# Eight transposes of the identity ahead of the first transposes of the normalised input, in a four-layer attention and convolution kernel

## The chip, the cores and the metric

The kernel runs on one core of a Trainium2 chip. The metric is device time in microseconds (us) of one execution; lower is better. The core's engines each work through their own list of instructions: TensorE (PE, with its weight loads shown as PEld), VectorE (DVE), ScalarE (ACT), GpSimd (POOL) and SyncE (SP), which issues most of the transfers (DMA). They wait for each other through semaphores.

## The reference

The input `x` is 2048 rows of 512 in bf16. Four residual layers follow each other, two of a kind:

```python
x = x + _A_ref(_layernorm(x, axis=-1), A_wqkv, A_wo)
x = x + _B_ref(_layernorm(x, axis=-1), B_A_re, B_A_im, B_B_re, B_B_im, B_C_re, B_C_im, B_log_dt, B_Dskip)
x = x + _A_ref(_layernorm(x, axis=-1), A_wqkv, A_wo)
x = x + _B_ref(_layernorm(x, axis=-1), B_A_re, B_A_im, B_B_re, B_B_im, B_C_re, B_C_im, B_log_dt, B_Dskip)
```

`_A_ref` is attention with 32 heads of 16 over a window of 8 keys that lie 2 rows apart: projections to q, k and v, logits, a softmax over the 8 keys, the weighted sum of v, and a projection by `A_wo`. `_B_ref` builds, from complex parameters, a kernel K of 2048 taps for each of the 512 channels, convolves each channel of its input with it (through a transform of length 4096 in the reference), and adds the input times `Dskip`.

## The kernel before

All of the order is written by hand: a string of letters for each stage (`ORDERK`, `CORE0`, `ORDER0`, `ORDERF`, `CORE1`, `ORDER1`) names the operations one after the other, and each engine gets its instructions in that order. Everything is unrolled; there is no loop on the chip.

In order of time the stages are:

- `k_gen` (to about 105 us). VectorE and ScalarE build the tables of the convolution kernel. TensorE first transposes the parameters (`turned_by`, line 1048), then has nothing until the input is normalised. Between the table work stands the front of the first attention layer: ScalarE takes the sums of the input block `x_blk`, normalises it (line 195), TensorE transposes it (`turn`, line 1213) into a PSUM tile `pt`, ScalarE copies that to `xnT` (line 1216), and TensorE projects k and q (`proj`, line 1223).
- `core` of the first attention layer. Each of the 16 blocks of 128 rows has a product of the attention weights with v on VectorE (`pv_mult`, line 472, tile `pav`), a sum of it on TensorE by 64 small multiplies with the identity (`pv_sum`, line 497, tile `po`), a copy on ScalarE (line 499), the output projection (`out_proj`, lines 506 and 508) and its copy with the sums of the next layer norm (lines 514 and 145).
- The convolution of the first layer as a transform in two steps (`FftB`: lines 810, 821, 828, 865, 877, 891, 895, 939 to 945).
- The same two for the second layers (`ORDERF` and `CORE1` up to about 343 us, then `ORDER1`).

The change touches `turn` inside `k_gen`. It is called eight times, for four blocks b and two halves d of their columns, each time with a new tile from the PSUM pool `ps_tr` of two buffers. The calls are listed under the key `t` of the operations. The identity `ident` is made by GpSimd at the start and already serves the transposes of the parameters.

Every multiply or transpose on TensorE is two instructions, a weight load and the multiply. Line 1213 waits for ScalarE's line 195 row by row.

Of the kernel before, what the change touches and what calls it, by code (L numbers as in the profile page):

```python
# [74 lines left out]
"""  # L75
ROWS0 = (0, 2, 1, 3, 4, 5, 6, 7, 8, 9, 10, 11, 12, 13, 14, 15)
ROWS1 = (0, 2, 1, 3, 4, 5, 6, 7, 8, 9, 10, 11, 12, 13, 14, 15)
NCOL = (4, 3)
ENGK = dict(b="AAAAAAAAAAAAAAAAA", y="AAAAAAAAAAAA", z="AAAA", e="AAAAAAAA", K="AAAAAAAAAAAAAAAA", Q="AAAAAAAA", x="AAAAAAAAAAAAAAAA")
STATD = (3,)  # L80
# [6 lines left out]
def build_a_consts(nc, cpool, tpool, c):  # L87
# [14 lines left out]
    sv = tpool.tile([4, 4, H], I32, name="iota_slot")  # L102
    mc = tpool.tile([4, max(NCOL), W], I32, name="iota_slot_mask")
    ind = cpool.tile([P, NDT * H], BF16, name="ind32")

    def iotas():
        nc.gpsimd.iota(u[:], pattern=[[-16, 8]], base=0, channel_multiplier=1)
        nc.gpsimd.iota(mv[:], pattern=[[1, NA], [-2, W]], base=0, channel_multiplier=0)
        nc.gpsimd.iota(sv[:], pattern=[[-1, 4], [0, H]], base=0, channel_multiplier=1)
        nc.gpsimd.iota(mc[:], pattern=[[4, max(NCOL)], [-2, W]], base=0, channel_multiplier=1)  # L110
        nc.gpsimd.memset(ind[:], 0.0)

    def rest():
# [12 lines left out]
        nc.gpsimd.tensor_scalar(slot[:], sv[:], 0, None, ALU.is_equal)  # L126
        keep = cpool.tile([4, max(NCOL), W], BF16, name="slot_mask")
        nc.gpsimd.tensor_scalar(keep[:], mc[:], 0, -1e9, ALU.is_lt, ALU.mult)
# [71 lines left out]
class LayerA:  # L200


    def __init__(self, tc, nc, consts, lnst, A_wqkv, A_wo, layer, xnT, nq):
        self.tc, self.nc, self.c, self.lnst, self.layer = tc, nc, consts, lnst, layer
        self.ncol = NCOL[layer]
        self.ctx = ExitStack()
# [152 lines left out]
    def core(self, x_sb, u, lnp, order, ev, nprod=0):  # L359
# [9 lines left out]
        with ExitStack() as c2:  # L369
# [184 lines left out]
            blocks = [(q,) for q in range(4)]  # L554
            rows = [(a,) for a in (ROWS1 if l else ROWS0)]
            ops = dict(
# [450 lines left out]
def k_gen(tc, nc, a_consts, ins, kd, la, x_v, lnst, zero, b_consts):  # L1007
# [3 lines left out]
    with ExitStack() as ctx:  # L1011
# [10 lines left out]
        ident = la.c["ident"]  # L1022
# [51 lines left out]
        p_im = turned_by("A_im", by_dt)  # L1074
        p_re = turned_by("A_re", by_dt)
        nc.scalar.mul(nat(turn), p_im, 1.0 / TWO_PI)
        nc.vector.tensor_scalar(t1[:], turn, MAGIC, None, ALU.add)
        nc.vector.scalar_tensor_tensor(turn, t1[:], MAGIC, turn, ALU.subtract, ALU.subtract)
        nc.vector.scalar_tensor_tensor(t2[:], turn, -1.0, turn, ALU.mult, ALU.max)
        nc.scalar.activation(nat(a_re), p_re, ACT.Exp)  # L1080
# [6 lines left out]
        for name, copy in (("B_re", nc.scalar.copy), ("B_im", nc.scalar.copy)):  # L1087
            b = sp.tile([P, 4 * P], BF16, name="in_" + name)
# [119 lines left out]

        def turn(b, d):
            pt = xps[b, d] = la.ps_tr.tile([P, 2, 4, P], BF16, name="pt")  # L1210
            for di in range(2):
                for a in range(4):
                    nc.tensor.transpose(pt[:, di, a, :], xb[b][:, a, (2 * d + di) * P:(2 * d + di + 1) * P], ident[:])  # L1213
# [119 lines left out]
        def calls(f, *args):  # L1333
            return [lambda a=a: f(*a) for a in args]

        def chain(*fs):
# [6 lines left out]
            b=[f for k in range(12) for f in calls(power, (k,)) + (calls(power_neg, (k,)) if 3 <= k <= 7 else [])],  # L1343
# [9 lines left out]
            d=calls(x_load, (2,), (3,)), E=calls(la.front_ext, *((b, "dma") for b in range(3))),  # L1353
# [257 lines left out]
```

## Time and profile before

| | us |
|---|---|
| median of 3 runs | 389.48 |
| lowest and highest | 389.33, 390.03 |
| the profiled execution | 390.78 |
| its span, from its first to its last instruction | 389.0 |

The runs of the table's first two rows are without a profile; the third is the one that the profile's rows come from. The activity of the engines in 40 equal slices of the span, 9.7 us each, in tenths:

```profile
PE   3000267999999999999998999999999999997894
DVE  6999999999999999999999989979999999989984
ACT  7999999898578799999999998764675889989993
```

TensorE has little to do in the first 50 us and much from 65 us on; VectorE is nearly full all along. In rows of the timeline the columns are the start, the time to the end of the group, the engine, the line, the operation with its tiles and sizes, the count, and in brackets the idle time before with what ended it. Rows of the chain that ended last have a start, a length, the engine, tile and line. "issue" is time in which an engine waited for nothing that the profile shows.

### The profile page before, as it was taken

How to read it: one execution, taken by the hardware profiler on the slowest of the kernel's cores; microseconds unless marked ns; L12 is line 12 of the kernel's file. 1: busy time of each engine (PE TensorE's matmuls, PEld its weight loads, DVE VectorE, ACT ScalarE, POOL GpSimd, SP SyncE). 2: the span in 40 equal slices, each digit the busy share in tenths (PEclk: the TensorE clock that was granted, in tenths of full speed). 3: DMA queues.
4: the chain of work that ended last, by engine and by line, in shares of the span. 5: the costliest groups of instructions: out<-in, count | busy, mean ns of one | idle time of the engine just before them, and what ended most of it. 6: DMA issues, size and time to landing. Idle time of an engine off the chain costs nothing.

```text
span 389.0 us, 14544 instructions
## 1 busy us (share of the span) xinstructions
PE 324.6 (83%) x6361; PEld 220.7 (57%) x6361; DVE 369.1 (95%) x439; ACT 338.0 (87%) x581; POOL 63.3 (16%) x97
## 2 busy tenths in 40 slices
PE   3000267999999999999998999999999999997894
PEld 2000125757634455666887898544446666677894
DVE  6999999999999999999999989979999999989984
ACT  7999999898578799999999998764675889989993
POOL 9400980000290000001531200200000010000000
PEclk9999999999999999999999999999999999999999
DMA  7951822114025556287575733077303274404515
GB/s 206 405 172 18 86 73 75 36 35 96 16 66 167 169 168 189 77 231 234 213 273 224 273 112 111 3 264 224 95 0 97 70 237 144 157 3 148 182 55 168
DMA packets 68302, 54.16 MB, mean 139 GB/s; under 512 B 33545, under 2 KB 58670, under 8 KB 67982
## 3 DMA queue, kind: packets, MB, share of 16 engines
q1 hardware_dynamic: 66566, 48.70, 42.4%
q0 software_dynamic: 1664, 4.52, 3.1%
q8 instruction: 50, 0.82, 0.9%
q14 instruction: 14, 0.11, 0.1%
q10 hardware_dynamic: 8, 0.00, 0.0%
HBM read 30.15 MB, written 13.24 MB: 112 GB/s over the span
## 4 chain that ended last, share of the span: by engine, by line
PE 46%; ACT 20%; issue 3%; SPq 2%; DMA 1%; DVE 0%; ACTq 0%
PE pq L398 7%; ACT ub L877 5%; PE pq L223 5%; ACT a1s L810 5%; PE po L497 4%; PE pp L282 4%; PE pq L508 3%; PE L L350 3%; PE pb L821 2%; SPq L597 2%; PE pb L891 2%; PE L L424 2%; PE pb L895 2%; PE pb L940 2%; PE pb L941 1%
## 5 line engine op out<-in xcount | busy, mean ns | idle before, releaser
L472 DVE TENSOR_TENSOR pav<-attn,v_ext 128x4096 bf16<-128x4096 bf16 (+1 forms) x34 | 72.2, 2158 | 0.2 <-PE po L497 0.2
L342 DVE TENSOR_TENSOR prod<-qT,kT_ext 128x4096 bf16<-128x4096 bf16 x29 | 65.4, 2287 | 1.9 <-ACT qT L225 0.6
L1213 PE MATMUL pt<-ident,x_blk 128*128 128x128 bf16 x64 | 6.3, 241 | 39.4 <-ACT x_blk L195 39.4
L1127 DVE TENSOR_TENSOR A_t<-A_t,pow_t 128x1024 bf16<-128x1024 bf16 (+4 forms) x46 | 38.1, 869 | 0.1
L497 PEld LDWEIGHTS <-pav 64*128 64x128 bf16 x1984 | 31.1, 95 | 12.1 <-issue 7.0
L497 PE MATMUL po<-ident,pav 64*128 64x64 bf16 x1984 | 34.7, 190 | 0.7 <-issue 0.5
L508 PE MATMUL pq<-wop,oT 128*128 128x512 bf16 x128 | 32.8, 379 | 0.0
L877 ACT CAST ub<-pb 128x1024 bf16<-128x1024 f32 x32 | 31.7, 1116 | 0.0
L828 PE MATMUL pb<-a1s,w_sb 128*128 128x64 bf16 x768 | 27.7, 193 | 3.6 <-ACT a1s L810 1.9
L810 ACT CAST a1s<-pb 128x1024 bf16<-128x1024 f32 x30 | 29.4, 1054 | 1.4 <-PE pb L821 1.2
L1223 PE MATMUL pp<-xnT,kT_ext 128*128 128x512 bf16 x96 | 26.2, 402 | 4.9 <-ACT kT_ext L1228 2.1
L398 PE MATMUL pq<-wv,xnT 128*128 128x512 bf16 x128 | 30.2, 379 | 0.0
L1213 PEld LDWEIGHTS <-x_blk 128*128 128x128 bf16 x64 | 4.8, 107 | 41.7 <-ACT x_blk L195 40.5
L828 PEld LDWEIGHTS <-w_sb 128*128 128x128 bf16 x768 | 24.9, 98 | 6.0 <-issue 4.3
L400 ACT CAST v_ext<-pq 128x512 bf16<-128x512 f32 x32 | 18.6, 586 | 11.1 <-PE pq L398 10.9
L223 PE MATMUL pq<-xnT,kT_ext 128*128 128x512 bf16 x96 | 24.2, 380 | 0.0
L1285 PEld LDWEIGHTS <-A_t 128*64 128x64 bf16 (+1 forms) x512 | 21.6, 103 | 3.8 <-DVE A_t L1127 0.2
L1285 PE MATMUL pk<-B_t,A_t 128*64 128x84 bf16 (+1 forms) x512 | 23.5, 201 | 0.1
L810 DVE CAST a1s<-pb 128x1024 bf16<-128x1024 f32 x18 | 21.4, 1218 | 1.5 <-PE pb L821 1.1
L499 ACT CAST oT<-po 128x512 bf16<-128x512 f32 x31 | 17.8, 573 | 3.6 <-PE po L497 3.6
L398 PEld LDWEIGHTS <-xnT 128*128 128x128 bf16 x128 | 11.9, 98 | 15.5 <-issue 2.3
L508 PEld LDWEIGHTS <-oT 128*128 128x128 bf16 x128 | 12.5, 98 | 12.6
(262 smaller groups left out, 888.5 us busy)
## 6 DMA issues: line engine op xcount, KB each, us to landing
w_sb<-w_dram SPq DMA_DIRECT2D x64, 128.0 KB, 3.3
w_dram<-xnT SPq DMA_DIRECT2D x1, 4096.0 KB
kf_ring<-kf_dram SPq DMA_DIRECT2D x13, 256.0 KB, 3.9
kf_ring<-kf_dram SPq DMA_DIRECT2D x26, 128.0 KB, 4.3
v_ext<-v_ext SPq DMA_DIRECT2D x4, 784.0 KB, 6.0
x_blk<-in_A_x_dram SPq DMA_DIRECT2D x4, 512.0 KB, 5.3
kT_ext<-in_A_wqkv_dram SPq DMA_DIRECT2D x4, 512.0 KB, 13.1
x_sb<-in_A_x_dram SPq DMA_DIRECT2D x4, 512.0 KB, 6.8
```

Of the source, the lines that this page charges most:

```text
L223: nc.tensor.matmul(pq[:], lhsT=self.wqk[:, dt, ft * P:(ft + 1) * P], rhs=self.xnT[:, dt, q * 512:(q + 1) * 512], start=(dt == 0), stop=(dt ...
L342: nc.vector.tensor_tensor(pr, self.qT[q][:, ft].unsqueeze(1).to_broadcast([P, W, 4, P]), kap, ALU.mult)
L398: nc.tensor.matmul(pp[:], lhsT=xnT[:, dt, a * P:(a + 1) * P], rhs=wv[:, dt, :], start=(dt == 0), stop=(dt == NDT - 1))
L472: nc.vector.tensor_tensor(pv[:, i], attn[:, n % 4].unsqueeze(2).to_broadcast([P, W, DH // parts, H]), vap, ALU.mult)
L497: nc.tensor.matmul(po[:, h, 0, i * nt + ft, :], lhsT=pvf[rows, i, w, ft * P:(ft + 1) * P], rhs=ident[rows, rows], start=(w == 0 and ft + i ...
L508: nc.tensor.matmul(pw[:], lhsT=oT[:, ftp, :], rhs=self.wo[:, ftp, :], start=False, stop=(ftp == NDT - 1))
L810: (self.nc.scalar.copy if eng == "act" else self.nc.vector.tensor_copy)(dst, src)
L828: nc.tensor.matmul(p2[:, j, :], lhsT=self.w2[:, ec * EC + j, :], rhs=a1s[:, ec * EC + j, :], start=True, stop=True)
L877: nc.scalar.copy(ub[:], p2)
L1127: return lambda: nc.vector.tensor_tensor(*args)
L1223: nc.tensor.matmul(pps[kind, b, ft][:], lhsT=la.wqk[:, dt, c:c + P], rhs=la.xnT[:, dt, b * 512:(b + 1) * 512], start=(dt == 0), stop=(dt = ...
L1285: nc.tensor.matmul(o, lhsT=lhs, rhs=Bt[:, ri, c * CH + ql].rearrange("p b g -> p (b g)"), start=(not half and j % 4 == 0 and ri == 0), sto ...
```

## The change

Ahead of the eight transposes of the first call of `turn`, eight transposes of the identity are put into the first place of the same tile, which the first real transpose then overwrites. Nothing reads them.

```diff
+IDLE = 8
...
         def turn(b, d):
             pt = xps[b, d] = la.ps_tr.tile([P, 2, 4, P], BF16, name="pt")
+            for _ in range(IDLE if (b, d) == (0, 0) else 0):
+                nc.tensor.transpose(pt[:, 0, 0, :], ident[:], ident[:])
             for di in range(2):
                 for a in range(4):
```

TensorE's list grows by 16 instructions; the other engines' lists keep theirs in the same order.

## The prediction

> **What bounds the kernel now.** I read the busy shares first, then the chain that ended last, then the costliest groups for the line that changes.
>
> ```profile
> PE 324.6 (83%) x6361; PEld 220.7 (57%) x6361; DVE 369.1 (95%) x439; ACT 338.0 (87%) x581; POOL 63.3 (16%) x97
> PE 46%; ACT 20%; issue 3%; SPq 2%; DMA 1%; DVE 0%; ACTq 0%
> L1213 PE MATMUL pt<-ident,x_blk 128*128 128x128 bf16 x64 | 6.3, 241 | 39.4 <-ACT x_blk L195 39.4
> q8 instruction: 50, 0.82, 0.9%
> ```
>
> Three engines are nearly full and hand the bound to each other: VectorE is busy 95% of the span, TensorE carries 46% of the chain, ScalarE 20%. The third row is the group the change touches: TensorE idles 39.4 us ahead of the transposes of the normalised input, waiting for ScalarE. The fourth is what the change can reach later: 50 instruction packets, 0.82 MB, so 16.4 KB each. TensorE has 6361 multiplies and 6361 weight loads, 12722 instructions; 12722 / 50 = 254 for a packet. So one packet a block of about 256 TensorE instructions. Every engine's other instructions stand in the same order after the change, but all 16 added ones (a weight load with each transpose) push the later code 16 places on, so each block now ends 8 multiplies earlier in the program.
>
> **The direct cost.** The next view is TensorE's order of time around the inserted place, and the engine totals of the stretch.
>
> ```profile
> 7.02 0.60 PE L1048 MATMUL pt<-dt_diag,raw_C_im 128*128 128x128 bf16 x4 [0.76 <-DMA raw_C_im<-in_B_C_im_dram]
> 45.02 0.29 PE L1213 MATMUL pt<-ident,x_blk 128*128 128x128 bf16 x1 [37.40 <-ACT x_blk L195]
> 47.14 1.57 PE L1213 MATMUL pt<-ident,x_blk 128*128 128x128 bf16 x13 [0.42 <-ACT x_blk L195]
> 45.00:54.20 9.20, 6.44 (x26) 3.02 (x27) 9.20 (x16) 9.20 (x18) 9.20 (x1) 1.00 0.62 111
> ```
>
> The eight transposes read only the identity, so they carry no wait: they start when the last transposes of `raw_C_im` are through, at about 7.6 us, and not at 45 us. Thirteen transposes back to back take 1.57 us, 0.12 us each, so eight take about 1 us and end near 8.7 us. The next work on TensorE starts at 45.02 us. Cover: 36 us of idle. Direct cost 0; without that cover it would be 1 us. They write a tile whose first reader waits for the later real transposes, so nobody waits for them; no DMA is added, and no queue is passed.
>
> **The indirect cost: where the blocks end.** I searched the bursts of equal small multiplies for a gap that no wait explains. There are two. The view is the chain in order of time, then the timeline: TensorE's weight loads and multiplies, and two rows of ScalarE behind them.
>
> ```profile
> 310.10 1.04 PE po L497 x64
> 311.14 0.89 PE L L354 x32
> 312.03 0.13 PE L L332
> 312.16 0.55 PE L L459 x8
> 312.71 0.63 PE po L497 x36
> 313.35 0.47 issue
> 313.82 0.58 PE po L497 x28
> ...
> 322.89 0.48 ACT oT L499
> ...
> 323.41 1.11 PE po L497 x64
> 324.52 0.54 PE L L424 x2
> 325.06 0.22 PE pq L506
> 325.27 0.86 PE pq L508 x4
> 326.14 1.04 PE po L497 x63
> 327.17 0.03 issue
> 327.20 0.20 PE po L497
> ```
> ```profile
> 310.03 0.26 PEld L497 LDWEIGHTS <-pav 64*128 64x128 bf16 x14 [0.42 <-DVE pav L472]
> 312.65 0.70 PE L497 MATMUL po<-ident,pav 64*128 64x64 bf16 x36
> 313.82 0.58 PE L497 MATMUL po<-ident,pav 64*128 64x64 bf16 x28 [0.47 <-issue]
> 326.07 1.33 PE L497 MATMUL po<-ident,pav 64*128 64x64 bf16 x64
> 314.44 0.58 ACT L499 CAST oT<-po 128x512 bf16<-128x512 f32 x1 [0.68 <-PE po L497]
> 328.62 0.60 ACT L514 ACTIVATE x_sb<-pq 128x512 bf16<-128x512 f32 x1 [0.19 <-PE pq L508]
> ```
>
> One burst of 64 halts between its 36th and 37th multiply; another between its 63rd and 64th. In the program's list the two late weight loads stand 768 = 3 x 256 places apart, so both open a block. The sizes: the first burst spans 313.82 + 0.58 - 312.65 = 1.75 us against the 1.11 of the burst at 323.41, so 0.64 us are lost; the second 1.33 - 1.11 = 0.22. Together 0.86 us.
>
> When is the block asked for? Counting 128 multiplies back from the 37th of the first burst (36, 8, 1, 32, and 51 of the 64) leads to the 14th of the burst before, just behind the wait for line 472 that opens it; 313.82 - 310.03, its first load, is 3.79 us. For the second, 63 + 4 + 1 + 2 = 70, so 58 back into the burst at 323.41, its 7th; 327.20 - 323.41 = 3.79 as well. I read: a block is asked for as the one before it opens, and is usable about 3.8 us later.
>
> After the change each of these points lies 8 multiplies earlier. First halt: the asking point moves from the 14th to the 6th of the burst at 310.03, still behind its wait, so the block comes at the same time or, at 1.04 / 64 us a multiply, 0.13 us sooner; the need comes 0.13 us sooner. The halt stays, between 0 and 0.13 us dearer. Second halt: the 7th of its burst minus 8 lies ahead of the burst, in the wide multiplies of L508, before the wait that ended at 323.41. Their row:
>
> ```profile
> 322.74 0.59 PE L508 MATMUL pq<-wop,oT 128*128 128x512 bf16 x2
> ```
>
> The third of those four starts at 322.74, and the asking point is at its weight load or earlier: at least 0.67 us more lead against 0.13 us less, so the 0.22 us halt goes. What is late next there is ScalarE: 0.19 us of its idle time in front of line 514 at 328.62 hangs on it, so I credit 0.2, at worst 0.
>
> New halts I look for where two successive block starts come closer than 3.8 us. Counting blocks off the same way, three new starts fall into these groups of weight loads:
>
> ```profile
> 226.01 0.19 PEld L895 LDWEIGHTS <-t 64*128 64x128 bf16 x8
> 229.61 0.18 PEld L895 LDWEIGHTS <-t 64*128 64x128 bf16 x7
> 233.03 0.21 PEld L891 LDWEIGHTS <-t 128*128 128x128 bf16 x3
> ```
>
> They stand 3.6 and 3.4 us apart, 7.0 for two blocks against 7.6. Already before the change the spacing there was as tight (3.6 and 3.4) with no halt, since the sequencer runs some multiplies ahead; each new start comes 0.3 to 0.45 us earlier. I charge 0.2 us, nearer to the unhalted rows of before than to the shortfall, between 0 and 0.45.
>
> The sum: 0 (transposes) + 0.1 (first halt) - 0.2 (second) + 0.2 (near 230 us) = +0.1 us, with bounds of -0.2 and +0.6. Against its own run this is 389.0 us of span plus 1.8 around it, 390.8 in all; the runs without that profile have a median of 389.48, 1.3 us lower. The difference carries over: 389.6.
>
> The Trainium skill, "Runtime: NRT & Kernel Launch", section on instruction fetch mechanics, says that TensorE's code comes in blocks of 256 instructions, with 2048 held on the engine, and that a boundary's cost is mostly hidden. The block size agrees with the 254 of the trace; hidden boundaries do not agree with the halt of 0.47 us. By that rule the change would cost 0 and the time would be 389.5.
>
> **Rivals.** *Slower: a block fetch that arrives late behind other transfers.* Place: the burst of line 497 at 142.25 us. Rows of the DMA by queue in 140 to 144 us and in 141.4 to 141.6, then TensorE and ScalarE there:
>
> ```profile
> q8 instruction: 1, 0.02, 1.8%
> q8 instruction: 1, 0.02, 36.9%
> 143.08 0.16 PEld L497 LDWEIGHTS <-pav 64*128 64x128 bf16 x6
> 144.38 0.81 PE L508 MATMUL pq<-wop,oT 128*128 128x512 bf16 x3
> 144.15 0.56 ACT L499 CAST oT<-po 128x512 bf16<-128x512 f32 x1
> ```
>
> The packet takes 0.018 x 16 x 4.0 = 1.2 us and begins within 141.4 to 141.6, so it ends near 142.7, though the block before opened 128 multiplies ahead of 144.6, near 138.8. Before the first halt the packet's rows are
>
> ```profile
> q8 instruction: 1, 0.02, 2.7%
> q8 instruction: 1, 0.02, 81.3%
> ```
>
> for 310 to 313 and 311.0 to 311.1 us: 0.027 x 16 x 3.0 = 1.3 us from about 311.0, so it ended 1.5 us before 313.82. If a block is usable 1.5 us after its packet and not 3.8 after its request, the one at 142.7 serves from 144.2. Before, it began with the second multiply of the group of L508 at 144.38, so it was needed at 144.6; now it begins in the group of loads at 143.08: a halt of 1.1 us. Line 499 of ScalarE waits for that burst at 144.15, so about half is hidden: +0.5 us; with the 0.45 near 230 us and 0.35 for two more blocks as short as the second old halt, at 0.2 each, +1.3, 390.8. It decides once more than 0.6 us of new halts reach the end. For it: three engines nearly full, so little absorbs. Against it: the chain at 143 us runs on ScalarE.
>
> *Faster: both old halts go.* If blocks are asked for earlier than I count (the sequencer reads past a wait), 8 places could free the first as well: -0.86 us, 388.6. ScalarE idles 0.68 us at 314.44 in front of line 499 for that halt, so most would reach the end. Against it: the asking point stays behind its wait.
>
> *Faster: the extra transposes warm TensorE's clock.* The transposes at 47.14 take 0.12 us each, and a TensorE kept busy before might run them and the multiplies behind them faster. But VectorE and ScalarE are busy 9.20 of 9.20 us there, so a faster TensorE gives 0: 389.5. The Trainium skill, "TensorE: Matmul & The Clock Gate", part 1, says the clock rises after some 3.4 us of sustained work and falls after as long idle; with 36 us of idle between, it too gives nothing.
>
> **How the numbers follow.** About 0.2% (0.8 us) is what a measurement of this kernel can tell from no change. Forecast, blocks shifted with gains and losses that cancel: 0.49, own range 389.0 to 390.2 (the bounds of the sum and the spread of the runs, 389.33 to 390.03). Slower by late blocks: 0.30. Faster, both halts gone: 0.18. Warm clock: 0.03, no change in time. So faster 0.18, same 0.52, slower 0.30. The range reaches down to the faster rival, 388.5, and up past the slower, 391.0.
>
> **What would show it.** Right: eight transposes near 7.7 us; line 1213 still starting at about 45.0; the halt at 313 between the 28th and 29th multiply of its burst; none in the burst at 326. Wrong: a new unexplained gap in a burst of line 497 near 143 us or of lines 821 to 941, no halt at 313, or any move of the stretch before 60 us. A time outside 388.5 to 391.0 would mean that something other than the block ends is at work.

## The result and the profile after

| | before | after |
|---|---|---|
| median, us | 390.03 (389.33 to 391.22, 9 runs) | 392.0 (390.6 to 393.48, 9 runs) |
| the profiled execution, us | 390.78 | 392.0 |
| its span, us | 389.0 | 390.2 |

Side by side on one chip the ratio is 1.0037 (1.0019 to 1.0055): slower by about 1.4 us, and the median of 392.0 lies outside the predicted range of 388.5 to 391.0. The page of the changed kernel, in the order of the first fence of the prediction: busy shares, chain, the costliest group that the change touches (line 1213 has become 1216), instruction packets.

```profile
PE   4000268999999999999998999999999998997894
PE 322.2 (83%) x6320; PEld 222.2 (57%) x6369; DVE 369.1 (95%) x439; ACT 338.3 (87%) x581; POOL 63.3 (16%) x97
PE 45%; ACT 16%; issue 4%; DMA 3%; DVE 2%; SPq 2%; DVEq 0%; ACTq 0%
L1216 PE MATMUL pt<-ident,x_blk 128*128 128x128 bf16 x64 | 6.7, 259 | 38.6 <-ACT x_blk L196 38.6
q8 instruction: 50, 0.82, 0.9%
```

VectorE did the same work in the same 369.1 us. In the chain "issue" grew from 3% to 4%: time in which an engine waits for nothing that the profile shows. DMA (1% to 3%) and DVE (0% to 2%) grew too; but two of the three long DMA pieces of the chain lie at 163 and 174 us, where, as the next rows show, nothing was late yet, and at the third, at 210 us, nothing more was lost. The number of packets is still 50. (6369 weight loads are 8 more than before; some multiply records are missing.)

The transposes and the work behind them, in TensorE's order of time (line numbers of the changed kernel are 1 higher up to line 1210, 3 higher behind):

```profile
6.66 1.06 PE L1213 MATMUL pt<-ident 128*128 128x128 bf16 x8
45.02 0.29 PE L1216 MATMUL pt<-ident,x_blk 128*128 128x128 bf16 x1 [37.30 <-ACT x_blk L196]
```

They took 1.06 us, were over by 7.72 (a microsecond sooner than forecast, as the transposes of `raw_C_im` did not wait for their load in this execution), and the first real transpose starts at 45.02 us as before. VectorE's and ScalarE's instructions start within 0.02 us of their times in the kernel before until 188 us. So the direct cost is 0, and everything came later. The first place is at 188 us: ScalarE there before, then after, then TensorE's weight loads and multiplies after.

```profile
185.96 4.79 ACT L810 CAST a1s<-pb 128x1024 bf16<-128x1024 f32 x5
```
```profile
185.96 2.82 ACT L811 CAST a1s<-pb 128x1024 bf16<-128x1024 f32 x3
189.43 1.93 ACT L811 CAST a1s<-pb 128x1024 bf16<-128x1024 f32 x2 [0.65 <-PE pb L822]
187.57 0.26 PEld L829 LDWEIGHTS <-w_sb 128*128 128x128 bf16 x7
188.37 0.33 PEld L829 LDWEIGHTS <-w_sb 128*128 128x128 bf16 x9 [0.54 <-issue]
188.37 0.45 PE L829 MATMUL pb<-a1s,w_sb 128*128 128x64 bf16 x10 [0.45 <-issue]
```

Sixteen equal loads are cut after the seventh, the gap is "issue", and ScalarE, which copied five tiles without a break before, stands 0.65 us waiting for the multiplies behind it. From here VectorE and ScalarE run 0.60 us late. The second place is at 230 us, the third between 310 and 329:

```profile
228.92 1.45 PEld L896 LDWEIGHTS <-t 64*128 64x128 bf16 x95
230.62 0.09 PEld L896 LDWEIGHTS <-t 64*128 64x128 bf16 x1 [0.24 <-issue]
```
```profile
310.95 0.99 PEld L498 LDWEIGHTS <-pav 64*128 64x128 bf16 x64 [0.42 <-DVE pav L473]
313.56 0.99 PEld L498 LDWEIGHTS <-pav 64*128 64x128 bf16 x64
319.14 0.99 PEld L498 LDWEIGHTS <-pav 64*128 64x128 bf16 x64 [0.43 <-DVE pav L473]
322.42 0.32 PEld L509 LDWEIGHTS <-oT 128*128 128x128 bf16 x2
323.65 0.11 PEld L509 LDWEIGHTS <-oT 128*128 128x128 bf16 x2 [0.92 <-issue]
326.84 0.87 PEld L498 LDWEIGHTS <-pav 64*128 64x128 bf16 x55 [0.42 <-issue]
328.20 0.20 PEld L498 LDWEIGHTS <-pav 64*128 64x128 bf16 x9 [0.49 <-issue]
```

At 230 us 0.31 more reach VectorE (0.92 in all). At 313.56 the burst that was cut into 36 and 28 before is whole: that halt is gone, and ScalarE's delay falls to 0.27 there. But the out projection (line 509) is now cut in its middle at 323.65, and the burst behind it after its 55th load; ScalarE is back at 0.92, and 0.20 more at 327.5 make 1.13 us at the end, beside 1.2 of the span.

Where did these blocks wait? The DMA by queue in three windows: from the opening of the block before the 188 us halt to the packet, the 0.1 us in which the packet begins, and the 0.1 us of the packet for the block of 313 us.

```profile
q1 hardware_dynamic: 188, 1.01, 92.5%
```
```profile
q8 instruction: 1, 0.02, 60.0%
q1 hardware_dynamic: 6, 0.00, 3.4%
```
```profile
q1 hardware_dynamic: 28, 0.02, 75.2%
q8 instruction: 1, 0.02, 56.7%
```

The first is 182.66 to 185.9 us: no instruction packet, the engines 92.5% full with other transfers. The second is 185.9 to 186.0: those are all but over (3.4%), and the packet starts; it takes 0.60 x 16 x 0.1 = 0.96 us, ends at 186.94, and the block opens 1.43 us later. The third is 310.1 to 310.2: this packet begins 0.9 us before the block ahead of its own opens (311.00, the sixth load of the burst at 310.95).

### The profile page after: what moved, and what is told of

Its sections match the earlier page's. It is cut to its first block, busy times and chain, and to the rows that moved or that the text cites. A ratio compares the mean times of both kernels' runs of the same rounds, so it can differ in the third digit from the quotient of the medians.

```text
span 390.2 us, 14511 instructions
## 1 busy us (share of the span) xinstructions
PE 322.2 (83%) x6320; PEld 222.2 (57%) x6369; DVE 369.1 (95%) x439; ACT 338.3 (87%) x581; POOL 63.3 (16%) x97
## 4 chain that ended last, share of the span: by engine, by line
PE 45%; ACT 16%; issue 4%; DMA 3%; DVE 2%; SPq 2%; DVEq 0%; ACTq 0%
PE pq L399 7%; PE po L498 5%; PE pq L224 5%; PE pq L509 4%; ACT a1s L811 4%; PE pp L283 3%; ACT ub L878 3%; PE L L351 3%; PE pb L892 2%; PE pb L822 2%; PE L L425 2%; DMA w_sb<-w_dram 2%; PE pb L896 2%; PE pb L941 2%; SPq L598 2%
## 5 line engine op out<-in xcount | busy, mean ns | idle before, releaser
L509 PE MATMUL pq<-wop,oT 128*128 128x512 bf16 x120 | 31.5, 379 | 3.3 <-issue 2.5
L224 PE MATMUL pq<-xnT,kT_ext 128*128 128x512 bf16 x90 | 23.4, 380 | 0.4 <-issue 0.2
```

Of the source, the lines that this page charges most:

```text
L224: nc.tensor.matmul(pq[:], lhsT=self.wqk[:, dt, ft * P:(ft + 1) * P], rhs=self.xnT[:, dt, q * 512:(q + 1) * 512], start=(dt == 0), stop=(dt ...
L509: nc.tensor.matmul(pw[:], lhsT=oT[:, ftp, :], rhs=self.wo[:, ftp, :], start=False, stop=(ftp == NDT - 1))
```

## The experiments

From the trace a short table can be made for each block: when the one before it opened (its weight load, every 256th TensorE instruction), when its packet began and ended, when it opened itself. Every halt told of below falls on such an opening. Three theories:

- **Position.** What counts is which instructions open blocks; a block is usable a set time (1.2 us or more) after its own packet, and the packet may be late.
- **The transposes cost.** Eight more instructions, or a warmer or busier TensorE, slow something.
- **Chance of one execution.** The difference is how transfers fell in this execution; the program's positions only say where it can hurt.

Each ratio is to runs of the kernel before on the same chip; medians of different rows may come from different chips. Three kernels that were run once each stand outside the table.

| kernel | median, us | ratio (95%) |
|---|---|---|
| 128 transposes | 391.45 | 0.9999 (0.9977 to 1.0020) |
| 8, as in the change | 391.3 | 1.0019 (0.9999 to 1.0040) |
| the kernel before | 390.76 | 0.9991 (0.9971 to 1.0012) |
| 8, `g` later in the string | 392.07 | 1.0028 (1.0007 to 1.0048) |
| 14 | 391.12 | 1.0040 (1.0023 to 1.0056) |
| 106 | 391.08 | 1.0049 (1.0026 to 1.0072) |
| 8, in the second layer | 390.74 | 1.0023 (1.0012 to 1.0033) |
| 64 | 390.86 | 1.0020 (0.9999 to 1.0041) |
| 120 | 389.56 | 0.9993 (0.9969 to 1.0016) |

**A whole block of transposes.** `IDLE = 128`: 256 instructions, so every block opens where it did before.

> 128 transposes instead of 8: 256 added instructions, one whole block, so all later code lies at the same place within its block as before the change. Theory (where the blocks end decides): the time is that of the kernel before, 390.0 us within 0.5, and halts without a wait fall at the same multiplies as before (37th of 64 in the burst of line 497 near 313, 64th near 327) or at other block ends of before, none at the four places of the changed kernel. Rival (the transposes themselves cost, by their time, by the clock or by what they write): 16 times as many cost at least what eight do, so 391.4 us or more. They need 128 x 0.107 = 13.7 us and have 36 us of idle.

The ratio is 0.9999 with sixteen times the added work. Weight loads of this kernel around 313 us:

```profile
312.86 0.58 PEld L498 LDWEIGHTS <-pav 64*128 64x128 bf16 x36
314.27 0.46 PEld L498 LDWEIGHTS <-pav 64*128 64x128 bf16 x28 [0.83 <-issue]
```

The cut is back after the 36th, exactly the place of the kernel before. One of 0.3 stands at 169 us, also at a block end of the kernel before, and the burst at 326 us is whole. Until 173 us VectorE's and ScalarE's instructions start within 0.03 us of their times in the kernel before, with all 128 transposes over by 17 us. So in this trace the transposes themselves cost nothing, and position holds. The time by itself would not show that: the median of 391.45 lies above the 391.3 of the next run, on the same chip, and the two intervals overlap.

**The changed kernel again**, unaltered.

> The changed kernel once more, unaltered. Theory A (a block's halt is fixed by the program): the halts near 188.4, 230.6, 323.7 and 328.2 us come back with 0.6, 0.3, 0.8 and 0.56 us, and the time is 1.0037 times that of before. Theory B (a halt depends on how long the block's packet stood behind other transfers in that execution): every halt lies at a block end and ends 1.2 to 1.7 us after its packet, but which block ends halt differs in part, above all the one at 188.4, where the packet began 3.3 us after the block before opened, against 1.3 in the kernel before.

```profile
187.61 0.52 PEld L829 LDWEIGHTS <-w_sb 128*128 128x128 bf16 x16
322.91 0.11 PEld L509 LDWEIGHTS <-oT 128*128 128x128 bf16 x2 [0.47 <-issue]
```

No halt at 188 us this time; its packet began 0.85 us after the block before opened, not 3.32. Those at 230, 323 and 327 are there (smaller), and new ones of 0.3 at 143 and 234. So positions say where a halt can be, the execution says which are, and how large: the ratio of 1.0019 is lower than the first 1.0037, though the intervals overlap. In this trace VectorE ends only 0.11 us later than in the first trace of the kernel before.

**The kernel before again**, the floor of such a comparison.

> The kernel before, unaltered: how far two comparisons of one program agree, and which of its halts come back. Theory A: 0.64 us near 313 and 0.22 near 327 again and no other. Theory B: the halts at 313 and 327 mostly again, since there the block is asked for late, with others now and then; ratio 1.000 within 0.002.

```profile
312.80 0.58 PEld L497 LDWEIGHTS <-pav 64*128 64x128 bf16 x36
314.50 0.46 PEld L497 LDWEIGHTS <-pav 64*128 64x128 bf16 x28 [1.11 <-issue]
326.75 0.99 PEld L497 LDWEIGHTS <-pav 64*128 64x128 bf16 x64 [0.42 <-issue]
```

The same halt is larger here (1.2 us between the loads, against 0.7), and the other of the kernel before, in the burst at 326, is absent. VectorE ends 0.46 us later than in the first trace, so the second traces of the two kernels have the same span, 389.4 us: the 1.13 us above belong to one pair of executions. The ratio of 0.9991 shows that 0.1% means nothing.

**g_sb later, by its letter.** In the changed kernel `g`, the load of `g_sb` (1 MB), moves seven operations back in the string, to take it away from 183 us.

```diff
-g KD KA KA KA KA KD KD KA KA KD ...
+KD KA KA KA KA KD KD g KA KA KD ...
```

> The changed kernel with one transfer of 1024 KB (g_sb from g_dram) issued seven steps later in the order of the first convolution. In the changed kernel it was issued at 181.6 us, just ahead of the packet that came late (186.0 to 186.9) for the block of the halt at 188.4. Theory (contention): that packet begins within 2 us of its block's predecessor again, the halt near 188 goes, and the time falls by up to 0.6 us against the changed kernel, 391.4 or less. Rival (the halt comes from the place of the block end alone): it stays and the time is 392.0.

The load did not move. SyncE's queue does not wait for the other engines' places in the string, and those seven operations put nothing on SyncE's list. The load's issue in the changed kernel, in this run, in the changed kernel again and in the kernel before:

```profile
181.55 0.36 SPq L1502 DMA_DIRECT2D g_sb<-g_dram  x1
181.63 0.36 SPq L1502 DMA_DIRECT2D g_sb<-g_dram  x1
182.68 0.36 SPq L1502 DMA_DIRECT2D g_sb<-g_dram  x1
183.47 0.37 SPq L1499 DMA_DIRECT2D g_sb<-g_dram  x1
```

So the run is the changed kernel once more, and its 1.0028 is a third measurement of it. The packet was late again: DMA by queue from 182.5 to 185.9 us,

```profile
q1 hardware_dynamic: 235, 1.08, 96.6%
```

it began 3.06 us after its block's forerunner opened, and there was a halt of 0.25. Whether the packet waits for `g_sb` was not tested, since no run moved that load. But the 14 traces fall into two groups at this place. In seven of them `g_sb` was issued 1.11 to 1.87 us before the forerunner opened, and the packet began 2.53 to 3.32 us after that opening. In the other seven it was issued at most 0.51 us before the opening, or after it, and the packet began 0.66 to 1.32 us after. That makes `g_sb` the likely transfer, and the time of its issue the likely difference between the two executions of the changed kernel.

**14 transposes.**

```diff
-IDLE = 8
+IDLE = 14
```

> 14 transposes instead of 8: block ends lie 14 multiplies earlier than before the change, 6 earlier than with eight. Theory (a block is asked for some 18 to 22 instructions before the running one reaches the end of the block before it, and is usable about 3.5 us later): counted through the trace of before, only one place is short, 0.1 to 0.3 us near 233; none near 313, 323 or 328. So 389.9 to 390.5 us beside a kernel before of 390.4, ratio 0.997 to 1.000. Rival (time rises with the number of added transposes): 14 cost more than 8, ratio 1.005 or more.

A miss: 1.0040. Cuts of 0.23 to 0.42 us stood at four block openings, at 188, 230, 234 and 322 us, so that my forecast of which places would be short, made from block distances alone, does not work.

**106 transposes**, chosen to put block ends where the bursts are shortest.

> 106 transposes: by the same count the worst place for the block ends. Theory: halts near 300 (0.5 to 0.8 us), 313.5 (1.2 to 1.9), 328 (0.1 to 1.2) and 378 (0.9 to 1.2), together 2.7 to 5.4 us, of which a third to two thirds reach the end: ratio 1.003 to 1.008. Rival (the transposes cost by their number): between 8 and 128 added ones, ratio that of 128, 1.000.

```profile
313.37 0.90 PEld L498 LDWEIGHTS <-pav 64*128 64x128 bf16 x58
315.01 0.14 PEld L498 LDWEIGHTS <-pav 64*128 64x128 bf16 x6 [0.74 <-issue]
377.59 1.95 PEld L896 LDWEIGHTS <-t 64*128 64x128 bf16 x130
379.94 0.50 PEld L896 LDWEIGHTS <-t 64*128 64x128 bf16 x30 [0.39 <-issue]
```

Halts near 300, 314 and 379 us as forecast, smaller than I gave; none at 328, and one of 0.32 at 231 that I had not given. The ratio of 1.0049 lies within the forecast.

**The w_sb loads later, by their letters.** In `CORE1` all four `W` behind the last `t f`, to clear the DMA between 310 and 328 us.

```diff
-nPOSlWOOSPblWTxPSedPWOrSfOP...OSPWdfOPaSPOSfbPdOaStfOfSfatafO
+nPOSlOOSPblTxPSedPOrSfOP...OSPdfOPaSPOSfbPdOaStfWWWWOfSfatafO
```

> The changed kernel with all 32 loads of w_sb of the second layer issued behind the last copies of the attention, near 340 us, so that few transfers run from 305 to 330 us. The time is not the question: the convolution behind waits for the loads and should be 5 to 15 us longer. Theory (packets come late behind other transfers): the packets of the two blocks that halted at 323.7 and 328.2 begin within 1.0 us of the opening of the block before instead of 1.9 and 2.1, and the halts shrink from 1.0 and 0.6 to 0.3 or nothing. Rival (the delay is the engine's own): packets and halts as they were.

One run: 392.38 us. It says nothing on the question, for the same reason as with `g`: the loads began at 309.49 us, as in the changed kernel (308.60). As one more trace of the changed kernel it had the halts at 188, 323 and 328.

**Eight transposes later on.** The kernel before with the eight in front of the first transposes of the second attention layer, at 239.7 us, so that only the blocks behind that move.

```diff
+            for _ in range(8 if (b, dp) == (0, 0) else 0):
+                nc.tensor.transpose(pt[:, 0, 0, :], self.c["ident"][:], self.c["ident"][:])
```

> The kernel before with the eight transposes put ahead of the first transposes of the second attention layer (near 240 us) instead of the first: only blocks after that shift. TensorE is busy there, so up to 8 x 0.06 = 0.5 us of their own time. Theory: no halt near 188, 230 or 234 beyond what the kernel before shows, none near 313, and the two near 323 and 328 as in the changed kernel. Time: from 0.2 us (the end's share of those two halts in the changed kernel's trace) to 0.7 us with the transposes, ratio 1.0005 to 1.002. Rival (the first layer's places carry nothing, all of the loss is late): ratio 1.003 or more.

The halts are those of the changed kernel in the part that moved (0.81 at 322.85, 0.31 at 327.13; none at 313) and none of it in the part that did not (143, 188, 230, 234). Position holds again. The ratio, 1.0023, is a little above what I gave. Not all of it need be halts: TensorE is busy here, the eight take 0.45 us of it, and from 242 us ScalarE runs 0.33 us later than in the kernel before, with no cut at a block opening near.

**The same loads held back in earnest.** The order of the run before, and ahead of the first load a small transfer that reads rows which ScalarE writes late:

```diff
+    def w2_held():
+        if not held:
+            held.append(nc.sync.dma_start(hold[:], x_sb[0:1, 10, 0:256]))
+        w2_next()
```

> The changed kernel with the w_sb loads of the second attention layer held back: ahead of them SyncE issues a small transfer that reads row block 10 of x_sb, which ScalarE writes at about 332 us, so that nothing but instruction packets moves from about 310 to 332 us. The loads then come later than their readers want them, so the time is longer by up to some 10 us; the question is only the stretch of 310 to 332 us. Theory (a block is usable 1.2 to 1.7 us after its own packet, and the packet is late behind other transfers): the packets there begin at most 1.1 us after the block before opened (1.90 and 2.07 in the changed kernel), the halt of 1.02 at 323.6 shrinks to 0.3 or less and the 0.58 at 328.2 goes. Rival (a block is usable a fixed 3.8 us or so after it is asked for, whatever else moves): both halts stay within 0.2 us of their size.

The loads started at 335.33 us. Nothing but instruction packets moved from 316.9 to 330 us (the first row is TensorE's queue in that window; beside it stands only one packet of 0.01 MB on another instruction queue, q14); the second is 323.0 to 323.1. Then the weight loads:

```profile
q8 instruction: 3, 0.05, 1.5%
```
```profile
q8 instruction: 1, 0.02, 63.4%
```
```profile
322.13 0.99 PEld L498 LDWEIGHTS <-pav 64*128 64x128 bf16 x64 [0.43 <-DVE pav L473]
325.41 0.75 PEld L509 LDWEIGHTS <-oT 128*128 128x128 bf16 x4
329.37 0.99 PEld L498 LDWEIGHTS <-pav 64*128 64x128 bf16 x64 [0.42 <-issue]
```

The block of the 323 us halt opens within the four loads at 325.41, the next within the burst at 329.37, and neither is cut. The packet at 323.04 began 0.81 us after the block before opened at 322.23 (1.90 in the changed kernel), the next after 0.69 (2.07). Both halts went with the traffic: here lateness behind other transfers is shown, in one execution, by taking them away. In all five traces with the changed kernel's places and these loads (the changed kernel, again, the two runs with moved letters, and the next one) the 323 us place halted, and its packet began 1.39 to 1.90 us after the opening. The same run had a halt of 1.9 us at 145, with a packet 3.86 us late. (So its time, 397.02, is not only that of convolution weights loaded late: VectorE is 3.1 us behind the changed kernel at 158 us, long before these loads, 2.0 at 343 and 4.9 at 377.)

**More traffic in a quiet stretch.** 20 useless loads of 128 KB from 342.35 us on.

```diff
+        nc.sync.dma_start(hold[:], x_sb[0:1, 15, 0:256])
+        for c in range(20):
+            nc.sync.dma_start(junk[:, c * 4:(c + 1) * 4, :], w2_dram[:, c * 4:(c + 1) * 4, :])
```

> The changed kernel with 20 useless loads of 128 KB, from one DRAM tensor to another, issued by SyncE from about 343.5 us on, into a stretch (343.5 to 353.5 us) in which the changed kernel moves nothing but instruction packets and has no halt. Theory: the packets there, 0.93, 0.83 and 0.56 us after the opening of the block before, come 0.5 to 1.5 us later, and the block that opens at 348.84 (1.86 us after the end of its packet, at least 1.2 are needed) halts by 0.1 to 0.9 us; perhaps the one at 353.1 too. Rival (fixed time): no new halt between 344 and 356 us.

DMA by queue from 343.4 to 353.5 us:

```profile
q1 hardware_dynamic: 1820, 1.66, 58.7%
q8 instruction: 3, 0.05, 2.0%
```

A miss. The three packets began 0.98, 1.28 and 0.96 us after the openings, 0.05, 0.45 and 0.40 later than without the traffic, and no block halted (the closest opened 1.85 us after its packet's end). In the run before, the held loads themselves filled this stretch to 77%, and packets came after 1.05 and 0.61 us. So traffic can hold a packet back, but a busy DMA does not always do so.

**64 and 120 transposes.** Half a block, and a block less 16 places: the other way round from the change.

> 64 transposes of the identity in place of 8: later instructions come 128 places on, half a block. Theory: other places of the program open blocks, none of those of the changed kernel or of the kernel before, so the halts are elsewhere, each 1.2 to 1.7 us after the end of that block's packet; the halts of 313, 323 and 328 us are gone. I cannot say which places halt instead; from the shifts tried so far the ratio is 0.999 to 1.005. Rival (the added instructions themselves cost): the ratio grows with their number, above that of 8 and of 106 (1.005).

> 120 transposes: later instructions come 240 places on, which leaves the block ends 16 places short of where they were before the change, the other way round from the changed kernel. Theory: halts near those of the kernel before, but 8 multiplies later in their bursts (313 us: the asking point falls further behind its wait, so the halt stays, 0.4 to 0.9); ratio 0.999 to 1.004. Rival (the added instructions themselves cost): 1.005 or more.

With 64 the cuts were 0.7 at 232.3 and 1.0 at 380.9 us, and 313, 323 and 328 were clear; the ratio is 1.0020. The rival, a cost that grows with the number, is refuted by 120, whose interval lies below that of 106; that of 64 overlaps it. With 120 I expected the halt at 313 to stay, and that was wrong:

```profile
310.44 0.99 PEld L498 LDWEIGHTS <-pav 64*128 64x128 bf16 x64 [0.42 <-DVE pav L473]
313.05 0.99 PEld L498 LDWEIGHTS <-pav 64*128 64x128 bf16 x64
325.82 0.99 PEld L498 LDWEIGHTS <-pav 64*128 64x128 bf16 x64 [0.42 <-issue]
```

Its packet came 0.61 us after the opening in the first burst, ended 1.46 us before the need, and the burst at 313.05 is whole. Both halts of the kernel before are gone; two cuts of under 0.3 stand at 189 and 300. VectorE ends 0.47 us earlier, and the span is 387.5 us. The ratio of 0.9993 still cannot be told from 1: it is the best of the shifts, and no proven gain.

## Why the prediction was wrong

The block that opens in the burst at 313 us shows, in six traces, what the steps missed. All times in us, worked out from the records:

| kernel | packet begins after the block before opens | it takes | from its end to the opening | block to block |
|---|---|---|---|---|
| before | 0.83 | 1.30 | 1.49 | 3.62 |
| before again | 1.77 | 0.93 | 1.44 | 4.14 |
| 128 | 1.63 | 0.94 | 1.28 | 3.85 |
| 120 | 0.61 | 0.89 | 1.46 | 2.96 |
| 8 (the change) | -0.89 | 0.91 | 2.94 | 2.96 |
| 8 again | -0.42 | 0.93 | 2.44 | 2.96 |

2.96 is what the multiplies between them took in the three traces without a halt; what is above it is the halt.

- **Direct cost 0: right.** The transposes lay in idle time, and nothing shifted before 188 us.
- **Block ends move by 8 multiplies and decide: right**, by the runs with 128 and with the transposes in the second layer.
- **"A block is asked for as the one before it opens, and is usable about 3.8 us later": wrong, and it carried the rest.** The two halts that agreed so well were put together differently: by the records 0.83 + 1.30 + 1.49 = 3.62 and 1.15 + 0.93 + 1.65 = 3.73 (lag of the packet, packet, time behind it). The two 3.79 were also not counted alike: the first from its burst's first weight load, the second from a row of the chain; from its first weight load, at 323.26, the second is 3.94. The time runs from the packet's end, and that moves. Over the 14 traces no block opened sooner than 1.20 us after its packet.
- **"The asking point stays behind its wait", so the first halt stays: wrong.** With the opening at the sixth load of the burst, as counted, the packet began 0.8 and 0.4 us before the wait had ended; with the opening at the 14th it began 0.8 to 1.8 us after that opening. So code was asked for at least ten instructions past a waiting one; eight multiplies earlier was enough. The faster rival had this, but the gain stayed inside: ScalarE kept it only until 323 us.
- **"The second halt goes", credit 0.2: wrong.** The step gave the block more lead by its asking point, but its packet was late (2.07 us), and the block ahead, which I had not listed, halted for the first time (1.02 us between loads where 0.22 is usual).
- **0.2 near 230 us: right in place and size** (0.31 reached the end).
- **The slower rival had the mechanism, not the place.** "Usable 1.5 us after its packet, and the packet late behind other transfers" is close to what the runs showed (1.20 us at the soonest), and its 390.8 with a chance of 0.30 was on the right side. At 143 us, where I put it, the changed kernel did not halt in its first trace (packet over at 141.77, opening at 143.18) and halted by 0.3 to 0.4 in others, by 1.9 in the run with the loads held back. It struck at 188 us, which no step looked at.
- **The mis-sized term** is that for new halts: +0.2 in the sum, 0.60 at 188 us, 0.31 at 230 and 0.20 at 327 in the trace. The first halt's 0.65 went and came back at 323. The sum was +0.1 and the trace has +1.13. (In the rival's sum, two blocks at 0.2 each are 0.4, not 0.35; nothing hangs on it.)
- **The base** carried some of the miss: the kernel before had a median of 390.03 in nine runs and not 389.48, so 0.55 of the 2.4 us between 389.6 and 392.0 are no effect of the change.
- **"A time outside 388.5 to 391.0 would mean that something other than the block ends is at work": wrong.** The time was outside, and the halts told of above all lie at block openings.
- **The warm clock** changed nothing: no instruction of VectorE or ScalarE started earlier before 188 us. With 120 transposes the mean granted clock in the records was 0.950, with none 1.000, and the run with 0.950 was the shorter one.

The prediction weighed the Trainium skill, "Runtime: NRT & Kernel Launch", section on instruction fetch mechanics, by which a block boundary's cost is mostly hidden. In no trace did more than 8 of the 50 boundaries halt, so "mostly" agrees; but those few made up the whole shift of 1.13 us in the first trace.

What stays open: which transfers hold a packet back (for the 183 us place `g_sb` is likely, not shown), and why the same loads did so at 320 us and hardly at 347. Nor is the size of the loss settled: three measurements of the changed kernel gave 1.0037, 1.0019 and 1.0028, and the ratio does not follow one trace closely (the kernel with the transposes in the second layer ends within 0.05 us of the kernel before on VectorE, at a ratio of 1.0023), since each execution has its own halts.

## What to carry to other kernels

In a long unrolled program, look for bursts of equal instructions that are cut without a wait, and see whether the cuts lie a constant number of instructions apart: then moving code, even in idle time, moves them, and a comparison of two kernels carries some 0.2 to 0.5% of this beside what the change is meant to do. A rule drawn from two such cuts in one trace is too little to price the next ones; measure the packet's begin and end for every block, and take the same kernel's second trace before trusting a place. An edit of this sort can be tested for itself by padding with a whole block, which put the halt at 313 us back to its place. And look in the trace whether an edit to the order of loads has moved the load: two here had not.

## What the runs showed of the hardware that was not expected

- TensorE's code arrives in packets of 16 KB, one for every 256 instructions, mostly 0.9 to 1.7 us long; the page counts that queue with the data's queues, as a share of the same 16 DMA engines. A block opened at the soonest 1.20 to 1.42 us (by trace) after its packet ended.
- A packet began, at the median of each trace, up to 0.6 us after the block before opened where the DMA was under 20% busy in the 1.5 us ahead of it, and 0.85 to 1.5 us after where it was over 60% busy, with single ones 3 us late and more (the latest 3.86). It can also begin before that opening, while TensorE still waits for other work: by 0.89 us at 311 in the changed kernel.
- The lateness of one and the same place varies between executions of one kernel: 3.32 and 0.85 us at 183 us in two runs of the changed kernel. Over 14 traces the lateness there goes with the issue of a load of 1 MB: 2.53 to 3.32 us where that load was issued more than a microsecond before the block ahead opened, 0.66 to 1.32 us elsewhere.
